# A convolution and SwiGLU kernel: a new order around the first pair of token blocks, and an earlier store in the last

## The chip, the cores and the metric

The kernel runs on one core of one Trainium2 chip. The metric is the device time of one execution, in microseconds (us). Times inside an execution are counted from the start of the profiled span.

## The reference

The input x has 8 sequences of 4096 tokens and 192 features. Eight heads of 24 features each have seven taps, a softmax over seven weights. The causal convolution feeds a SwiGLU feed-forward network without bias:

```python
w = softmax(weight)                                   # 8 heads x 7 taps
y[b, s, head] = sum(w[head, k] * x_pad[b, s + k, head] for k in range(7))
xn = y / sqrt(mean(y * y) + 1e-6) * rms_g             # per token, 192 features
g, val = xn @ w_gate, xn @ w_val                      # 192 -> 1536 each
out = (g / (1 + exp(-g)) * val) @ w_out               # 1536 -> 192
```

The network's weights arrive as 64-bit floats, so the kernel rebuilds 32-bit floats from pairs of words itself.

## The kernel before

**Pairs.** The 32768 tokens are worked through as 32 pairs, each of two blocks (g = 0, 1) of 512 tokens. The 1536 hidden features are 12 groups of 128, f, in four units of three. Pairs 1 to 31 use fewer, larger products: sums of weight tiles (`WSUM`, on GpSimd, written into `wf`) meet sums of inputs (`XSUM`, on VectorE, written into `xc`, L667), and the results are combined on ScalarE, VectorE and GpSimd. The same is done for the output product with sums of output weight tiles (`out_sums`, L811). Their instruction order is written out by hand in `ORDER`; a letter ahead of each name gives the engine.

**Pair 0** is computed plainly, because the sums are not there yet. `plain` makes 24 products (L981); for each of them ScalarE takes the silu of one half (L991, "silu step") and VectorE multiplies it with the other (L998, "value step"), which frees the two PSUM banks of the product. `outer` then multiplies with the output weights `wo_sb` (L1021): block 0 first takes f = 0 to 8 for four groups of 128 tokens, then f = 9 to 11, then block 1 takes all f. ScalarE and VectorE move the sums out (L1029, L1033).

**Conversion.** `convert` rebuilds weights in steps: three short operations on VectorE (L287, L291, L294), two or three on ScalarE (L298, L299, L302), one on VectorE (L304), and then, for the output weights, two on GpSimd (L310, L311), or, for the input weights, four more on VectorE up to L319. The output weights come in six parts of two f each; even parts share one scratch buffer, odd parts the other, so part i + 2 begins after part i has left GpSimd.

**The order around the first pair** is written in two tables. In `START` each letter takes one step: `p`, `s` and `v` a product, a silu and a value step of pair 0; `i` a step of an input weight unit; `o` and `O` a step of an even or odd output weight part; `c` a tap of pair 1's convolution; `n` a step of pair 1's normalisation (square on ScalarE, reduction on VectorE L470, factor on GpSimd L476 to L482, spread on VectorE L489, scaling on GpSimd L497); `w` a chunk of three or four weight sums (L345, L349). `LATER` places what is left between the instructions of `outer`, by a count in which one of its matmuls is 37.5; `t` stores pair 1's normalised input to DRAM from SyncE, and `fetch(1)` reads it back in the layout of the products. A place only fixes the order on each engine's queue; engines wait for each other by semaphores.

**Pair 2's** convolution in the version before is `conv(2)`: seven full-width taps on VectorE (L418, L420) into `y`. From pair 3 on `part_tap` is used: ScalarE puts the first tap of a third of the width into a free PSUM bank (L436), VectorE adds the others there (L444), the last one writing to `y`. After the last tap the buffer of x is free for the next `load`.

**The end of a pair.** Each half of a pair's output (rows of block 0, `st0`, and block 1, `st1`) is transposed on VectorE (`T11`, `T12`; `T21`, `T22`; L897) and stored with three transfers from SyncE (L947). In `ORDER`, `T21` and `st1` carry a "-": they run inside the following pair's list, and for the last pair behind `T11` and `st0`.

Of the kernel before, what the change touches and what calls it, by code (L numbers as in the profile page):

```python
# [19 lines left out]
def kernel(  # L20
# [10 lines left out]
    nc = tc.nc  # L31
# [391 lines left out]
        if k == K - 1:  # L423
            x_sb.pop(p)

    acc = {}

    def part_tap(p, k, j):

        cut = slice(j * T, (j + 1) * T)  # L430
        xf = x_sb[p][:].rearrange("p t a -> p (t a)")
        xk, w = xf[:, k * GS + j * T : k * GS + (j + 1) * T], tp[:, k : k + 1]
        if k == 0:
            h = SIDE[j]
            acc[p, j] = h, pick(h, False)
            nc.scalar.mul(bank(*acc[p, j])[:], xk, w)  # L436
            return
        at = bank(*acc[p, j])[:]
        dst = at
        if k == K - 1:  # L440
            if p not in ys:
                ys[p] = yp.tile([P, NJ, D], F32, name="y")
            dst = ys[p][:].rearrange("p j d -> p (j d)")[:, cut]
        nc.vector.scalar_tensor_tensor(  # L444
            out=dst, in0=xk, scalar=w, in1=at, op0=ALU.mult, op1=ALU.add
        )
        if k == K - 1:
            h, i = acc.pop((p, j))
            free[h].append(i)
            if not any(q == p for q, _ in acc):  # L450
                x_sb.pop(p)

    yn, st = {}, {}
# [237 lines left out]
    def put(at, do):  # L691
        heapq.heappush(line, (at, next(tick), do))
# [131 lines left out]
    class Pair:  # L824
        def __init__(self, p):
            self.p = p
            self.units = [Unit(u) for u in range(NU)]
            self.bk, self.tl, self.o_sb = {}, {}, {}
            self.line = self.products()

        def h(self, g, f):
# [80 lines left out]
        def do(self, eng, name):  # L912
            act, *at = name.split(".")
            p, n = self.p, NM * P
            if len(at) == 2:
                self.units[int(at[1])].do(eng, act, int(at[0]))
            elif at:
                self.sum(int(act[1]), int(at[0]), eng)
            elif act == "c1":
                self.open("Y", True)  # L920
                copy(eng, self.some("Y"), self.some("X"))
            elif act in ("s7", "c2"):
                t = self.tl[act] = tiles.pop(0)
                copy(eng, t[:, 0:n], self.some("Z" if act == "s7" else "X"))
            elif act in ("C22", "C21"):
                t = self.tl["s7" if act == "C22" else "c2"][:, 0:n]
                b = "X" if act == "C22" else "Z"
                nc.vector.tensor_tensor(out=t, in0=self.some(b), in1=t, op=ALU.add)
                if b == "Z":
                    self.close(b)  # L930
            elif act in ("T22", "T21"):
                t = self.tl.pop("s7" if act == "T22" else "c2")
                self.turn(t, 1, int(act[2]) - 1)
                tiles.append(t)
            elif act in ("T11", "T12"):
                b = "Y" if act == "T11" else "X"
                self.turn(self.bank(b), 0, int(act[2]) - 1)
                self.close(b)
            elif act in ("st0", "st1"):
                g = int(act[2])  # L940
                r = p * PT + g * T
                o = self.o_sb.pop(g)[:].rearrange("p a d -> p (a d)")
                o = o.rearrange("p (b d) -> p b d", d=HP)
                for c, rows, lo, hi in ((0, LOW, 0, 8), (1, UPP, 0, 8), (2, slice(0, P), 8, 12)):
                    n = T // (hi - lo)
                    to = out[r : r + T, c * HP : (c + 1) * HP].rearrange("(b p) d -> p b d", p=n)
                    nc.sync.dma_start(out=to, in_=o[rows, lo:hi, :])  # L947
            else:
                self.ahead(eng, act)

# [144 lines left out]
    def done(it):  # L1095
# [7 lines left out]


    START = (
        "XxxxxxXDdDdDTDdadTbTaTfbTakTakTakTkbkKkKkKkbkbfpoffpfsicpsvivOpsipiscvpisvpvwsicwpvs"
        "iwpvscwpsiwvpiscvipsvovpwispvswcipvwspsiwOvpsiwvipsvvpswopsvwcpsOnwonvpovnopOnOnopsOov"
    )
    LATER = (
        (-9, "t"), (54, "o"), (163, "s"),  # L1110
        (233, "s"), (294, "v"), (303, "s"), (463, "w"),
        (603, "v"), (679, "O"), (742, "w"), (802, "v"),
        (816, "O"), (1017, "O"), (1302, "w"), (1582, "w"), (1861, "w"), (2141, "w"),
        (2421, "w"),
    )
    conv_first(3, hot={4: 2, 5: 2, 6: 1})
    load(1)
# [29 lines left out]
    def later(it, *places):  # L1147
        for at in places:
            put(at, functools.partial(next, it, None))
# [10 lines left out]
        for at in places:  # L1160
            put(at, functools.partial(next, it, None))

    later(conv(2), *[c + 250 + 200 * i for i in range(K)], c + 1640)
    later(norm(2), c + 1650, c + 1850, c + 2050, c + 2420, c + 2440)
    later(place(2), c + 2450)
    xat = [c + i for i in (1660, 1730, 2060, 2130, 2200, 2270, 2340)]
    xat += [base + i for i in (2900, 2970, 3040, 3110, 3180)]
    for i, at in enumerate(xat[0 : len(XSUM)]):
        put(at, functools.partial(x_sum, i))
    later(out_sums(), *[base + 2600 + 60 * i for i in range(4 * NM)])  # L1170
    emit(float("inf"))
# [48 lines left out]
```

## Time and profile before

| | |
|---|---|
| three runs | 2630.27, 2627.51, 2630.32 us; median 2630.27 |
| profiled execution | 2624.07 us, of which the profiled span is 2622.2 |
| granted TensorE clock | 0.998 of full |
| PE, VectorE, ScalarE, GpSimd busy | 98%, 86%, 62%, 80% of the span |
| first plain product, first output product of pair 0, steady run of pair 1 begin | 38.9, 103.9, 145.45 us |
| last matmul ends | about 2614.7 us |

A line of a timeline gives start, duration, engine, source line, operation, output and inputs, count, and in brackets the idle time before it with what ended it. A line of the waits gives who waited for whom, the total, how often, and the longest. PE is TensorE, DVE VectorE, ACT ScalarE, POOL GpSimd, SPq the queue of SyncE. A matmul in 32-bit floats shows as two records.

### The profile page before, as it was taken

How to read it: one execution, taken by the hardware profiler on the slowest of the kernel's cores; microseconds unless marked ns; L12 is line 12 of the kernel's file. 1: busy time of each engine (PE TensorE's matmuls, PEld its weight loads, DVE VectorE, ACT ScalarE, POOL GpSimd, SP SyncE). 2: the span in 40 equal slices, each digit the busy share in tenths (PEclk: the TensorE clock that was granted, in tenths of full speed). 3: DMA queues.
4: the chain of work that ended last, by engine and by line, in shares of the span. 5: the costliest groups of instructions: out<-in, count | busy, mean ns of one | idle time of the engine just before them, and what ended most of it. 6: DMA issues, size and time to landing. Idle time of an engine off the chain costs nothing.

```text
span 2622.2 us, 71005 instructions
## 1 busy us (share of the span) xinstructions
PE 2579.8 (98%) x29002; PEld 1858.8 (71%) x29002; DVE 2268.0 (86%) x3606; ACT 1614.9 (62%) x2964; POOL 2091.7 (80%) x1693
## 2 busy tenths in 40 slices
PE   6899999999999999999999999999999999999998
PEld 4677777777777777777777777777757767777776
DVE  8988888888889888898888888888898888888875
ACT  5365556765557755567655567655577555676554
POOL 3988888777888777888788887778887778887776
PEclk9999999999999999999999999999999999999999
DMA  6313322323313233213233223233132332232210
GB/s 143 56 33 63 63 42 47 56 45 63 63 32 57 47 54 63 49 40 63 39 63 63 40 49 50 51 63 59 34 59 46 56 63 44 45 61 41 50 38 14
DMA packets 510659, 138.01 MB, mean 53 GB/s; under 512 B 482300, under 2 KB 484860, under 8 KB 510205
## 3 DMA queue, kind: packets, MB, share of 16 engines
q1 hardware_dynamic: 509772, 133.44, 27.1%
q8 instruction: 227, 3.72, 0.6%
q14 instruction: 100, 0.82, 0.1%
q10 hardware_dynamic: 560, 0.03, 0.0%
HBM read 83.87 MB, written 49.55 MB: 51 GB/s over the span
## 4 chain that ended last, share of the span: by engine, by line
PE 95%; POOL 1%; DMA 1%; DVE 1%; SPq 1%; issue 0%; ACT 0%; DVEq 0%; POOLq 0%
PE ps L753 62%; PE ps L882 33%; POOL wf L349 1%; PE ps L981 1%; DMA xh<-in_x_dram 0%; SPq L1119 0%; SPq L217 0%; DMA x<-in_x_dram 0%; POOL wo_sb L311 0%; DVE y L420 0%; DMA ht<-in_moe_w_val_dram 0%; DVE xc L667 0%; DVE ht L998 0%; DMA ht<-in_moe_w_gate_dram 0%; POOL xc L310 0%
## 5 line engine op out<-in xcount | busy, mean ns | idle before, releaser
L753 PE MATMUL ps<-xc,wf 64*128 64x512 f32 x4960 | 1253.8, 592 | 0.9 <-DVE xc L667 0.9
L753 PEld LDWEIGHTS ps<-xc,wf 64*128 64x128 f32 x4960 | 753.5, 186 | 315.5 <-issue 92.9
L753 PE MATMUL ps<-xb,wf 64*128 64x512 f32 x2480 | 711.2, 589 | 0.0
L705 ACT ACTIVATE tls<-ps 128x512 f32<-128x512 f32 (+1 forms) x636 | 365.7, 589 | 374.2 <-PE ps L882 203.1
L797 POOL TENSOR_TENSOR ht<-ht,tile 128x512 f32<-128x512 f32 x295 | 375.3, 1279 | 274.6 <-ACT tile L790 272.5
L705 ACT ACTIVATE tile<-ps 128x512 f32<-128x512 f32 x697 | 400.1, 594 | 269.3 <-PE ps L753 157.6
L753 PEld LDWEIGHTS ps<-xb,wf 64*128 64x128 f32 x2480 | 389.7, 187 | 146.5 <-issue 41.1
L705 ACT ACTIVATE ps<-ps 128x512 f32<-128x512 f32 (+1 forms) x651 | 366.9, 578 | 53.4 <-PE ps L882 38.8
L910 POOL TENSOR_TENSOR early<-ht 128x512 f32<-128x512 f32 x279 | 379.2, 1364 | 4.9
L797 POOL TENSOR_TENSOR ht<-ht,tls 128x512 f32<-128x512 f32 x201 | 255.2, 1277 | 72.5 <-ACT tls L790 70.6
L882 PE MATMUL ps<-ht,wo_sb 128*32 128x256 f32 (+1 forms) x6944 | 309.5, 326 | 0.0
L777 DVE TENSOR_TENSOR tile<-ps,tile 128x512 f32<-128x512 f32 x373 | 254.8, 686 | 56.3 <-PE ps L753 53.6
L444 DVE SCALAR_TENSOR_TENSOR ps<-xh,tp,ps 128x512 f32<-128x512 f32 x435 | 301.5, 744 | 1.0
L882 PEld LDWEIGHTS ps<-ht,wo_sb 128*32 128x32 f32 x6944 | 215.2, 110 | 93.2 <-POOL ht L797 22.7
L882 PE MATMUL ps<-ht,x 128*32 128x256 f32 (+1 forms) x5952 | 249.9, 326 | 0.6 <-issue 0.6
L910 POOL TENSOR_TENSOR ht<-ht 128x512 f32<-128x512 f32 x186 | 248.1, 1349 | 0.0
L790 ACT ACTIVATE tile<-tile 128x512 f32<-128x512 f32 x373 | 233.1, 629 | 12.5 <-DVE tile L777 12.5
L882 PEld LDWEIGHTS ps<-ht,x 128*32 128x32 f32 x5952 | 190.1, 110 | 54.7 <-issue 2.3
L777 DVE TENSOR_TENSOR ht<-ps,tls 128x512 f32<-128x512 f32 x311 | 211.5, 680 | 0.0
L777 DVE TENSOR_TENSOR ht<-ps,tile 128x512 f32<-128x512 f32 x309 | 210.1, 680 | 0.1
L777 DVE TENSOR_TENSOR tls<-ps,tls 128x512 f32<-128x512 f32 x247 | 169.2, 685 | 28.3 <-PE ps L753 26.1
L882 PE MATMUL ps<-early,x 128*32 128x256 f32 (+1 forms) x4464 | 193.1, 326 | 0.1
(129 smaller groups left out, 3164.6 us busy)
## 6 DMA issues: line engine op xcount, KB each, us to landing
xb<-xd SPq DMA_DIRECT2D x124, 384.0 KB
xd<-yn SPq DMA_DIRECT2D x248, 96.0 KB
out_dram<-o_sb SPq DMA_DIRECT2D x186, 128.0 KB
xh<-in_x_dram SPq DMA_DIRECT2D x192, 105.0 KB
xh<-in_x_dram SPq DMA_DIRECT2D x56, 98.4 KB
ht<-in_moe_w_gate_dram SPq DMA_DIRECT2D x12, 192.0 KB
ht<-in_moe_w_val_dram SPq DMA_DIRECT2D x12, 192.0 KB
tls<-in_moe_w_out_dram SPq DMA_DIRECT2D x8, 192.0 KB
```

The costliest lines, as they stand in the source:

```text
L349: nc.gpsimd.tensor_tensor(out=t[:, d, :], in0=t[:, a, :], in1=t[:, b, :], op=ALU.add if op == "add" else ALU.subtract,)
L444: nc.vector.scalar_tensor_tensor(out=dst, in0=xk, scalar=w, in1=at, op0=ALU.mult, op1=ALU.add)
L705: nc.scalar.activation(out=dst, in_=src, func=AF.Copy, scale=float(s))
L753: nc.tensor.matmul(out=self.new(v, h, True) if first else self.old(v, h), lhsT=wf[self.u][HALF[h], WAT[i], :], rhs=x_op(XOP[i])[HALF[h]], ...
L777: nc.vector.tensor_tensor(out=self.hv(v) if h else t[:], in0=self.old(v, h), in1=t[:], op=plus(s))
L790: nc.scalar.activation(out=t[:], in_=src[:], func=AF.Silu)
L797: engine[eng].tensor_tensor(out=self.hv(v), in0=src, in1=t[:], op=ALU.mult)
L882: nc.tensor.matmul(out=self.bank(b)[i * Q : (i + 1) * Q, at : at + n], lhsT=left, rhs=cols, start=fresh, stop=True, skip_group_check=True, ...
L910: engine[eng].tensor_tensor(out=dst, in0=a, in1=b, op=op)
L981: nc.tensor.matmul(out=bank(h, bks[h])[:], lhsT=wf[u][HALF[h], k * NF + f, :], rhs=xb[HALF[h], g, k, :], start=(k == 0), stop=(k == KP - 1 ...
```

## The change

Four things are changed. The order in `START` and `LATER`: one tap of pair 1 is moved behind the last conversion step of unit 1 and one behind that of unit 2; the value steps 18 to 23 come earlier among the conversions of the output weights; the weight sums from unit 2's second chunk on move behind all six parts of the output weights and then follow each other closely; the scaling of pair 1 moves behind output part 4. The convolution of pair 2 uses `part_tap`, with two thirds of the width first and the last third after them. The x sums of pair 1 are all placed ahead of the second evacuation group of `outer`, with pair 2's reduction and factor behind the seventh. For the last pair alone `T22`, `T21` and `st1` are done as soon as the second half's sum is there, and one transfer in three goes out from ScalarE.

The sets `ended` and `past` serve the bookkeeping while the instructions are emitted: x is released after the third part's last tap, and a name that was done early is skipped later.

```diff
@@ -423,7 +423,7 @@
         if k == K - 1:
             x_sb.pop(p)
 
-    acc = {}
+    acc, ended = {}, {}
 
     def part_tap(p, k, j):
 
@@ -447,7 +447,8 @@
         if k == K - 1:
             h, i = acc.pop((p, j))
             free[h].append(i)
-            if not any(q == p for q, _ in acc):
+            ended[p] = ended.get(p, 0) + 1
+            if ended[p] == len(SIDE):
                 x_sb.pop(p)
 
     yn, st = {}, {}
@@ -826,6 +827,7 @@
             self.p = p
             self.units = [Unit(u) for u in range(NU)]
             self.bk, self.tl, self.o_sb = {}, {}, {}
+            self.past = set()
             self.line = self.products()
 
         def h(self, g, f):
@@ -912,6 +914,9 @@
         def do(self, eng, name):
             act, *at = name.split(".")
             p, n = self.p, NM * P
+            if name in self.past:
+                return
+            self.past.add(name)
             if len(at) == 2:
                 self.units[int(at[1])].do(eng, act, int(at[0]))
             elif at:
@@ -928,6 +933,10 @@
                 nc.vector.tensor_tensor(out=t, in0=self.some(b), in1=t, op=ALU.add)
                 if b == "Z":
                     self.close(b)
+                    if p == PAIRS - 1:
+                        for name in ("T22", "T21", "st1"):
+                            if name not in self.past:
+                                self.do(eng, name)
             elif act in ("T22", "T21"):
                 t = self.tl.pop("s7" if act == "T22" else "c2")
                 self.turn(t, 1, int(act[2]) - 1)
@@ -944,7 +953,8 @@
                 for c, rows, lo, hi in ((0, LOW, 0, 8), (1, UPP, 0, 8), (2, slice(0, P), 8, 12)):
                     n = T // (hi - lo)
                     to = out[r : r + T, c * HP : (c + 1) * HP].rearrange("(b p) d -> p b d", p=n)
-                    nc.sync.dma_start(out=to, in_=o[rows, lo:hi, :])
+                    q = nc.scalar if c == 1 and p == PAIRS - 1 else nc.sync
+                    q.dma_start(out=to, in_=o[rows, lo:hi, :])
             else:
                 self.ahead(eng, act)
 
@@ -1103,15 +1113,13 @@
 
 
     START = (
-        "XxxxxxXDdDdDTDdadTbTaTfbTakTakTakTkbkKkKkKkbkbfpoffpfsicpsvivOpsipiscvpisvpvwsicwpvs"
-        "iwpvscwpsiwvpiscvipsvovpwispvswcipvwspsiwOvpsiwvipsvvpswopsvwcpsOnwonvpovnopOnOnopsOov"
+        "XxxxxxXDdDdDTDdadTbTaTfbTakTakTakTkbkKkKkKkbkbfpoffpfsicpsvivOpsipisvicpsvpvwsicwpvs"
+        "iwpvscwpsiwvpisvicpsvovpwispvswcipvwspsiwOvpsiwvipsvvpswopsvcpsvOnovnpsovnopsOvnOopsOoon"
     )
     LATER = (
-        (-9, "t"), (54, "o"), (163, "s"),
-        (233, "s"), (294, "v"), (303, "s"), (463, "w"),
-        (603, "v"), (679, "O"), (742, "w"), (802, "v"),
-        (816, "O"), (1017, "O"), (1302, "w"), (1582, "w"), (1861, "w"), (2141, "w"),
-        (2421, "w"),
+        (60, "t"), (163, "s"), (200, "v"), (250, "O"), (294, "v"), (330, "O"), (420, "O"),
+        (463, "w"), (564, "w"), (664, "w"), (764, "w"), (864, "w"), (964, "w"), (1064, "w"),
+        (1164, "w"), (1264, "w"),
     )
     conv_first(3, hot={4: 2, 5: 2, 6: 1})
     load(1)
@@ -1160,12 +1168,17 @@
         for at in places:
             put(at, functools.partial(next, it, None))
 
-    later(conv(2), *[c + 250 + 200 * i for i in range(K)], c + 1640)
-    later(norm(2), c + 1650, c + 1850, c + 2050, c + 2420, c + 2440)
+    for j in range(len(SIDE)):
+        put(c + 240 + 700 * (j // 2), functools.partial(part_tap, 2, 0, j))
+        for k in range(1, K):
+            at = c + 250 + 100 * k + 50 * j if j < 2 else c + 960 + 80 * k
+            put(at, functools.partial(part_tap, 2, k, j))
+    put(c + 1500, functools.partial(load, 3))
+    later(norm(2), c + 1510, c + 2300, c + 2310, c + 2420, c + 2440)
     later(place(2), c + 2450)
-    xat = [c + i for i in (1660, 1730, 2060, 2130, 2200, 2270, 2340)]
-    xat += [base + i for i in (2900, 2970, 3040, 3110, 3180)]
-    for i, at in enumerate(xat[0 : len(XSUM)]):
+    xat = [c + i for i in (1660, 1730, 2060, 2130, 2200, 2270, 2290)]
+    xat += [c + i for i in (2360, 2370, 2380, 2390)]
+    for i, at in enumerate(xat):
         put(at, functools.partial(x_sum, i))
     later(out_sums(), *[base + 2600 + 60 * i for i in range(4 * NM)])
     emit(float("inf"))
```

## The prediction

> **What bounds the kernel now.** I read the page's engine totals, then its chain of waits, then PE's waits over the whole run, then the timelines of the stretch in which those waits lie and of the last 20 us.
>
> ```profile
> PE 2579.8 (98%) x29002; PEld 1858.8 (71%) x29002; DVE 2268.0 (86%) x3606; ACT 1614.9 (62%) x2964; POOL 2091.7 (80%) x1693
> PE 95%; POOL 1%; DMA 1%; DVE 1%; SPq 1%; issue 0%; ACT 0%; DVEq 0%; POOLq 0%
> ```
>
> PE is the bound: the chain is PE from 145.45 us to 2614.7 us with no gap longer than 0.26 us. None of the edits removes a matmul, so time can only come from ahead of 145.45 us or from behind 2614.7 us. PE's waits say how much is there:
>
> ```profile
> PE ps L1021 <- POOL wo_sb L311: 3.3, 2, 1.7
> PE ps L1021 <- DVE ht L998: 3.0, 1, 3.0
> PE ps L981 <- DVE wf L319: 2.0, 2, 1.1
> PE ps L753 <- DVE xc L667: 0.9, 1, 0.9
> ```
>
> PE's own timeline places the L1021 and L753 waits between 105 and 146 us, where the first pair's output product runs:
>
> ```profile
> 103.92 1.46 PE L1021 MATMUL ps<-wo_sb,ht 64*128 64x192 f32 x8
> 108.34 1.89 PE L1021 MATMUL ps<-wo_sb,ht 64*128 64x192 f32 x18 [2.96 <-DVE ht L998]
> 111.90 9.70 PE L1021 MATMUL ps<-wo_sb,ht 64*128 64x192 f32 x116 [1.67 <-POOL wo_sb L311]
> 123.27 19.93 PE L1021 MATMUL ps<-wo_sb,ht 64*128 64x192 f32 x239 [1.68 <-POOL wo_sb L311]
> 145.45 1.13 PE L753 MATMUL ps<-xc,wf 64*128 64x512 f32 x4 [0.90 <-DVE xc L667]
> ```
>
> A record costs 83.5 ns here (9.70/116, 19.93/239). The first wait is for a PSUM bank: eight records go to the lower half, then the upper half needs the bank that value step 20 (L998) frees, and that step is late in VectorE's queue. The two others are for output weight parts 4 and 5 (f = 8 and f = 10). GpSimd's timeline shows what stands ahead of part 5:
>
> ```profile
> 110.23 1.62 POOL L311 TENSOR_TENSOR wo_sb<-xc 128x384 f32<-128x384 f32 x1
> 111.80 4.12 POOL L349 TENSOR_TENSOR wf<-wf 128x128 f32<-128x128 f32 x5
> 115.99 2.50 POOL L345 TENSOR_SCALAR wf<-wf 128x128 f32<-128x128 f32 x2
> 118.45 2.28 POOL L310 TENSOR_TENSOR xc<-xc,tls 128x384 f32<-128x384 f32 x1
> ```
>
> Seven weight sums, 6.3 us, run before it. On VectorE one short conversion runs beside GpSimd's scaling of pair 1 (L497, 102.83 to 105.67):
>
> ```profile
> 102.90 2.98 DVE L287 TENSOR_SCALAR xc<-tls 128x384 uint32<-128x384 uint32 x1 [1.83 <-POOL wo_sb L311]
> 106.88 0.35 DVE L294 TENSOR_SCALAR xc<-tls 128x384 uint32<-128x384 uint32 x1
> ```
>
> Alone such an operation takes 0.35 us. At the end, VectorE's and SyncE's timelines show the second half of the last pair's output waiting for the first:
>
> ```profile
> 2609.02 0.56 DVE L928 TENSOR_TENSOR tls<-ps,tls 128x384 f32<-128x384 f32 x1 [0.72 <-PE ps L882]
> 2614.80 0.65 DVE L897 STREAM_TRANSPOSE o_sb<-ps 128x256 f32<-128x256 f32 x2 [1.30 <-PE ps L882]
> 2615.37 0.59 DVE L897 STREAM_TRANSPOSE o_sb<-tls 128x256 f32<-128x256 f32 x2
> 2615.28 4.00 SPq L947 DMA_DIRECT2D out_dram<-o_sb  x6
> ```
>
> The data of that half are ready at 2609.6; its transpose runs at 2615.4 and its stores are the last three of six.
>
> **What the skill says.** The Trainium skill, "SBUF — State Buffer", section "SBUF: two separate sides": VectorE and GpSimd share a port pair as an exclusive lock held for a whole instruction, which an operation in a two-port mode or with two SBUF inputs needs. The trace agrees: 2.98 us instead of 0.35 while the 2.84 us scaling ran. So an operation moved on GpSimd also moves a block on VectorE. The Trainium skill, "DMA: Bandwidth & Descriptors", section "Issuing engines are not separate DMA queues": issuing from a second engine saves only issue time. The trace of before has all six stores on one queue, so nothing in it tests this.
>
> **The change part by part.** Durations are of the profiled execution: span 2622.2, own time 2624.07 us. The median of the runs is 2630.27, so 6.2 us is added at the end for whatever differs between the two.
>
> *One tap of pair 1 put behind the unit's last conversion, for units 1 and 2.* These remove the two L319 waits (0.86 and 1.15 us). VectorE is full there (20.0 of 20 us between 60 and 80), so the tap of 2.0 us only lands on the next value steps, and PE needs their banks: value step 3 ends at 58.1 instead of 58.0, and value steps 9 and 10 end about 0.9 us later. After unit 3's conversion both orders have done the same work. I take 0.4 us of the 2.0; bounds 0 and 1.3. The output product starts at 103.5 instead of 103.9.
>
> *Value steps 18 to 21 ahead of the conversions.* Step 20 now stands ahead of part 3's conversion, and its silu ahead of part 2's on ScalarE; it ends near 98.5. The 2.96 us wait goes. Late next is part 4: PE reaches f = 8 after 26 records, 2.2 us, at 105.7.
>
> *Weight sums and scaling behind parts 2 to 4.* Part 2 ends as before (102.9): it hangs on the factor step (L476 to L482, 2.5 us), still ahead of it. From there: GpSimd's first half of part 3, 1.0, blocks VectorE; three conversions of part 4, 1.05; L304, 0.55; then GpSimd's L311 of part 3, L310 and L311 of part 4, 1.0 each: 108.5. PE waits 2.8 us and resumes at 108.6 instead of 111.90: 3.3 us. Part 5 now has one operation, the scaling, ahead: 2.8 plus 2 x 1.0, done near 114, against PE's need at 118.4. The 1.68 us wait goes. PE would end the product at 108.6 + 358 x 0.0835 = 138.5.
>
> *What the later scaling holds up.* It runs from 108.9 to 111.8, not 102.8 to 105.7: 6.1 us later. SyncE's eight stores of pair 1 (5.2 us) and its four fetches wait for it in turn. The last fetch lands at about 121.9 before (DMA is busy until there), so at 128.0 now. VectorE's x sums cannot start earlier. Before, they start at 127.16, behind the taps, so here a hidden transfer comes into view.
>
> *Taps of pair 2 through PSUM.* Before: 1.17 + 1.97 + 1.95 + 8.75 = 13.8 us of VectorE. Now 18 at 0.743 (L444) = 13.4, and three first taps on ScalarE at 0.68 (L436), idle there. They start at 110 to 113 and end at 123 to 127, before the fetch lands, so they cost nothing; with the fetch on time they would be the limit. SyncE's load of pair 3 waits for them, behind the fetch in its queue; nobody needs it before 195.
>
> *x sums.* Eleven, 0.67 to 0.94 each, say 0.8: 8.8; one output addition 0.54; the reduction of pair 2, now in their midst, 1.75 + 0.24 + 0.22: 11.5 in all, so 139.5 (138.5 to 140.6). Then VectorE's spread (0.24) and one addition (0.53), which frees the upper bank that pair 1's second product takes: 140.35 instead of 145.45. **Front: 5.1 us**, bounds 3 and 7.
>
> *The 34 weight sums behind part 5.* At 0.47 alone and with 0.05 between, 17.7 us: 114 to 132, and 2 more beside the x sums. The factor step, 2.5 us, follows the reduction, which ends near 136.3, and the spread needs it at 139.5: no room to spare. Twelve output sums and the second scaling then end near 149.5; pair 1's first GpSimd product came 10.9 us after that pair's start, so about 151. Hidden.
>
> *Last pair.* Both transposes and the store move to 2609.6, where VectorE idles until 2612.8. After 2615.28 three stores are left instead of six: two on SyncE at 0.6 to 0.65, one on ScalarE, whose issues at the start took 0.39 to 0.72. Last issue ends near 2616.6 instead of 2619.28. **Tail: 2.6 us**, bounds 2.0 and 2.8. ScalarE has nothing behind it.
>
> Steady pairs keep their order, banks and durations: nothing. Sum: 7.7 us; profiled execution 2616.4, median 2630.27 - 7.7 = **2622.6**.
>
> **Rivals.** *PE stays the limit.* If the scaling is not blocked and the fetch lands at 126, pair 1 starts when the product ends, 138: front 7.4, in all 10.0, 2620.3. For it: before, the scaling took 2.84 us, unblocked, and 2 us gained on this chain suffice. Against: every step from 102 to 112 alternates on the shared lock. 15%.
>
> *The fetch becomes the bound.* Scaling or fetch come 3 us later still, because VectorE takes the lock between GpSimd's operations or load 3 shares the DMA engines (they are 0.7 to 0.9 busy with it in the trace): front 2.1, in all 4.7, 2625.6. 17%.
>
> *Slower: the weight sums hold VectorE.* They now stand ahead of pair 2's factor step, and VectorE's spread waits for that with the bank-freeing additions of pair 1 behind it. They took 0.84 each between 123.2 and 136.7, beside two-input taps, and up to 1.13. At 1.1 they end at 151.4; with 2.3 for the factor and 0.9 behind, pair 1 starts at 154.6, 9.1 late: 6.5 slower, 2636.8. It decides from 0.91 us each. Against it: the new taps read one input from PSUM, and the steady pairs' GpSimd sums beside them took 1.36 for 1.28. 8%.
>
> **Numbers.** The main case has 60%. A difference within 0.2%, 5.3 us, is about what a measurement of this kernel can tell from no change. Main and PE cases are faster by more (75%, and 2% of the fetch case), the rest of the fetch case lies within, the last is slower. The range goes from the PE case, less 2 for the scatter of a median, to the fetch case, plus 2: 2618 to 2627.5.
>
> **What would show it.** PE's timeline after: no wait for ht at L1021, one for part 4 of 2 to 3.5 us ending near 108.6, none for part 5; the scaling near 109; x sums idle until 128 for DMA; pair 1's second product near 140.4; six stores split three and three, the span ending 2.6 us behind what the front gives. Wrong would be: x sums starting by 125, a spread waiting on GpSimd beyond 141, or a wait in a steady pair.

## The result, and the profile after

| | before | after |
|---|---|---|
| median of 13 runs each (range), us | 2625.54 (2623.11 to 2630.32) | 2621.67 (2617.74 to 2623.89) |
| ratio of times, 95% interval | | 0.9981 [0.9973, 0.9989] |
| profiled execution; span, us | 2624.07; 2622.2 | 2620.28; 2618.4 |

The change makes the kernel faster by 1.1 to 2.7 thousandths, 2.9 to 7.1 us of 2625.5; the bound of 0.2% from the prediction lies inside this interval, so whether the gain exceeds it, as the prediction had it, stays open. The two medians lie 3.9 us apart, the two profiled executions 3.8. The predicted time was 2622.6. That it lies only 0.9 us from the measured median is luck, because two errors cancel: the median of 2630.27 that it started from came out at 2625.54 over more runs, and the gain of 7.7 us came out at 3.9 (5.0 by the ratio). From 2625.54 the same gain would have given 2617.8, just below the stated range.

In the kernel after, the lines of the file have moved: the products are L754 (L753 before), the output product of the pairs is L884 (L882), the plain product L991 (L981), `outer` L1031 (L1021), the x sums are L668 (L667), the value step L1008 (L998), spread, factor and scaling L490, L483 and L498, `outer`'s additions L1043, the last transposes L899 (L897), the stores L957 (L947).

Engine totals and shares of the chain, from the page of the kernel after:

```profile
PE 2580.3 (99%) x29002; PEld 1866.1 (71%) x29002; DVE 2265.0 (87%) x3617; ACT 1617.3 (62%) x2967; POOL 2079.0 (79%) x1693
PE 96%; DVE 2%; DMA 1%; issue 0%; POOL 0%; ACT 0%; SPq 0%; DVEq 0%; POOLq 0%; ACTq 0%
```

PE does the same 29002 records in 0.5 us more. GpSimd has fallen out of the chain (1% before). PE's waits over the whole run:

```profile
PE ps L884 <- issue: 3.3, 5, 1.4
PE ps L1031 <- POOL wo_sb L311: 2.5, 2, 1.4
PE ps L754 <- DVE xc L668: 1.1, 1, 1.1
PE ps L754 <- ACT tile L706: 0.3, 1, 0.3
```

The 3.0 us for `ht` and the 2.0 for `wf` are gone, and the waits for output parts fell from 3.3 to 2.5. But the steady pairs' output product (L884) now waits 3.3 us for nothing that the profile shows ("issue"), and there is a new wait of 0.3 us for ScalarE, in pair 3. Before, the only wait in the steady pairs was this one:

```profile
PE ps L882 <- issue: 1.9, 5, 0.8
```

PE's timeline between 102 and 142 us, after:

```profile
102.67 1.62 PE L1031 MATMUL ps<-wo_sb,ht 64*128 64x192 f32 x15
105.67 0.92 PE L1031 MATMUL ps<-wo_sb,ht 64*128 64x192 f32 x8 [1.38 <-POOL wo_sb L311]
107.72 29.36 PE L1031 MATMUL ps<-wo_sb,ht 64*128 64x192 f32 x355 [1.12 <-POOL wo_sb L311]
139.49 1.09 PE L754 MATMUL ps<-xc,wf 64*128 64x512 f32 x2 [1.07 <-DVE xc L668]
140.87 0.69 PE L754 MATMUL ps<-xc,wf 64*128 64x512 f32 x1 [0.28 <-DVE o_sb L1043]
```

PE stops for part 3 (1.38) and part 4 (1.12), not for part 5: 355 records run through in one piece, 82.7 ns each, from 107.72, where before they resumed at 111.90 and stopped again at 121.6. The second product of pair 1 reaches its upper half at 140.87 instead of 145.45. The other engines in the same stretch:

```profile
107.62 3.00 POOL L498 TENSOR_TENSOR yn<-y,s 128x1536 f32<-128x1536 f32 x1
107.80 3.03 DVE L294 TENSOR_SCALAR xc<-tls 128x384 uint32<-128x384 uint32 x1
110.64 6.36 SPq L633 DMA_DIRECT2D xd<-yn  x8
118.98 2.60 SPq L646 DMA_DIRECT2D xb<-xd  x4
129.61 0.93 DVE L668 TENSOR_TENSOR xc<-xb 128x512 f32<-128x512 f32 x1 [4.09 <-DMA xb<-xd]
138.67 0.68 DVE L668 TENSOR_TENSOR xc<-xc 128x512 f32<-128x512 f32 x1
140.13 0.25 DVE L490 STREAM_TRANSPOSE s<-s 128x64 f32<-128x64 f32 x1 [0.78 <-POOL s L483]
140.29 0.98 DVE L1043 TENSOR_TENSOR o_sb<-ps,o_sb 128x384 f32<-128x384 f32 x2
```

This is the chain that now sets pair 1's start: scaling, eight stores, four fetches, the first x sum after 4.09 us in which VectorE has nothing to do, the last x sum ending at 139.35, the spread after 0.78 us for the factor, and the addition that frees the bank. How much of the gain is still there one stage later is read from the chain of waits, at the step where pair 1's output product begins; first before, then after:

```profile
196.57 27.44 PE ps L882 x672
```

```profile
191.96 27.44 PE ps L884 x672
```

At this point after is 4.6 us ahead. VectorE's and the issuing queues' timelines at the end:

```profile
2607.68 0.64 DVE L899 STREAM_TRANSPOSE o_sb<-tls 128x256 f32<-128x256 f32 x2
2608.16 6.46 SPq L957 DMA_DIRECT2D out_dram<-o_sb  x4
2608.16 5.83 ACTq L957 DMA_DIRECT2D out_dram<-o_sb  x2
2612.87 0.65 DVE L899 STREAM_TRANSPOSE o_sb<-ps 128x256 f32<-128x256 f32 x2 [1.30 <-PE ps L884]
```

The second half's transpose runs 5.2 us ahead of the first half's instead of behind it, and four stores are on SyncE, two on ScalarE. The last matmul starts 5.88 us ahead of the span's end, before 7.74: 1.9 us. Front and tail make 6.5 us; the spans differ by 3.8. So 2.7 us were given back between 192 and 2612 us, in pairs whose work the change doesn't touch.

### The profile page after: what moved, and what is told of

It is laid out like the page before. It is cut to its first block, busy times and chain, and to the rows that moved or that the text cites. A ratio compares the mean times of both kernels' runs of the same rounds, so it can differ in the third digit from the quotient of the medians.

```text
span 2618.4 us, 71028 instructions
## 1 busy us (share of the span) xinstructions
PE 2580.3 (99%) x29002; PEld 1866.1 (71%) x29002; DVE 2265.0 (87%) x3617; ACT 1617.3 (62%) x2967; POOL 2079.0 (79%) x1693
## 4 chain that ended last, share of the span: by engine, by line
PE 96%; DVE 2%; DMA 1%; issue 0%; POOL 0%; ACT 0%; SPq 0%; DVEq 0%; POOLq 0%; ACTq 0%
PE ps L754 62%; PE ps L884 33%; PE ps L991 1%; PE ps L1031 1%; DMA x<-in_x_dram 0%; DMA xb<-xd 0%; DVE y L405 0%; DVE ht L1008 0%; DVE y L420 0%; DVE y L393 0%; DVE xc L304 0%; PE ps L594 0%; DVE wf L319 0%; ACT xb L614 0%; DVE xc L668 0%
## 5 line engine op out<-in xcount | busy, mean ns | idle before, releaser
L754 PE MATMUL ps<-xc,wf 64*128 64x512 f32 x4960 | 1252.8, 592 | 1.6 <-DVE xc L668 1.1
L754 PEld LDWEIGHTS ps<-xc,wf 64*128 64x128 f32 x4960 | 760.9, 186 | 308.1 <-issue 88.8
L754 PE MATMUL ps<-xb,wf 64*128 64x512 f32 x2480 | 709.1, 589 | 0.0
L754 PEld LDWEIGHTS ps<-xb,wf 64*128 64x128 f32 x2480 | 392.9, 187 | 141.2 <-issue 38.7
L444 DVE SCALAR_TENSOR_TENSOR ps<-xh,tp,ps 128x512 f32<-128x512 f32 x450 | 312.1, 745 | 1.7 <-ACT ps L436 0.6
L884 PE MATMUL ps<-ht,wo_sb 128*32 128x256 f32 (+1 forms) x6944 | 310.5, 326 | 0.0
L884 PEld LDWEIGHTS ps<-ht,wo_sb 128*32 128x32 f32 x6944 | 216.3, 110 | 92.8 <-POOL ht L798 23.5
L884 PE MATMUL ps<-ht,x 128*32 128x256 f32 (+1 forms) x5952 | 250.1, 326 | 0.4 <-issue 0.4
L884 PEld LDWEIGHTS ps<-ht,x 128*32 128x32 f32 x5952 | 190.5, 110 | 54.2 <-issue 1.6
L884 PE MATMUL ps<-early,x 128*32 128x256 f32 (+1 forms) x4464 | 193.5, 326 | 0.0
## 6 DMA issues: line engine op xcount, KB each, us to landing
out_dram<-o_sb SPq DMA_DIRECT2D x184, 128.0 KB
```

Of the source, the lines that this page charges most:

```text
L444: nc.vector.scalar_tensor_tensor(out=dst, in0=xk, scalar=w, in1=at, op0=ALU.mult, op1=ALU.add)
L754: nc.tensor.matmul(out=self.new(v, h, True) if first else self.old(v, h), lhsT=wf[self.u][HALF[h], WAT[i], :], rhs=x_op(XOP[i])[HALF[h]], ...
L884: nc.tensor.matmul(out=self.bank(b)[i * Q : (i + 1) * Q, at : at + n], lhsT=left, rhs=cols, start=fresh, stop=True, skip_group_check=True, ...
```

## The experiments

For every run I take four numbers from PE's records. *Front* is the time from the first plain product (38 to 39.5 us in all) to pair 1's first output product. *Start* is the time from the first plain product to the upper half of pair 1's second product, the point that the prediction put at 140.35. *Stops* is what lies between PE's records over their usual spacing, whatever its cause, from pair 1's first output product to the last matmul. *Tail* is the time from the last matmul's start to the end of the span. Where the start is left out, the product runs on without a gap at that point.

| run | own time, us | front | start | stops | tail |
|---|---|---|---|---|---|
| before | 2624.07 | 157.6 | 106.5 | 5.9 | 7.74 |
| after | 2620.28 | 153.1 | 102.0 | 8.5 | 5.88 |
| e1 tail only | 2622.68 | 157.4 | 106.3 | 7.3 | 5.88 |
| e2 front only | 2625.17 | 154.6 | 101.9 | 10.3 | 7.77 |
| e3 reduction early | 2617.41 | 150.5 | | 8.7 | 5.89 |
| e4 and load 3 later | 2620.32 | 150.5 | | 11.0 | 5.90 |
| e5 one queue | 2621.24 | 152.4 | 101.3 | 9.7 | 5.70 |
| e6 full taps | 2629.72 | 161.0 | 108.5 | 10.1 | 5.91 |
| e7 weight sums early | 2620.84 | 152.5 | 101.4 | 10.0 | 5.90 |
| e8 scaling early | 2624.62 | 155.7 | | 10.4 | 5.90 |
| e9 taps only | 2624.83 | 156.1 | | 7.9 | 7.65 |
| e10 swap undone | 2623.43 | 153.4 | 102.4 | 10.9 | 5.90 |
| e11 value steps undone | 2622.69 | 152.4 | 101.4 | 11.8 | 5.90 |
| e12 best | 2617.27 | 148.5 | | 9.7 | 5.91 |

After, e2 and e5 have the same front, instruction for instruction: it takes 152.4 to 154.6, and the start lies at 101.3 to 102.0. Part of e2's 154.6 is the clock, which was granted at 0.70 and 0.63 from 140 to 145 us where after had 1.00. So a difference of 0.7 us in the start, or of some 2 in the front, tells nothing unless a wait explains it.

**e1, the tail alone.** Before, with the hunks `past`, the early `T22`, `T21`, `st1`, and the second queue:

```diff
+                    if p == PAIRS - 1:
+                        for name in ("T22", "T21", "st1"):
...
-                    nc.sync.dma_start(out=to, in_=o[rows, lo:hi, :])
+                    q = nc.scalar if c == 1 and p == PAIRS - 1 else nc.sync
+                    q.dma_start(out=to, in_=o[rows, lo:hi, :])
```

> The order of before at the front, with only the last pair's early transposes, early store and the transfer from ScalarE. Theory (the gain is a sum of a front of 4.6 us and a tail of 1.9 us, less small stops of PE in the steady pairs that belong to the execution and not to the change): pair 1's first output product starts at 196.6 as before; from the start of the last transposes of block 0 to the end of the span 5.5 us instead of 7.4; time 1.9 us less, ratio 0.9993; the stops in pairs 2 to 31 add up to anything between 5 and 9 us. Rival (the change itself makes the steady pairs 2.6 us longer, through the banks that pair 2's taps leave behind): the stops are 5.8 us as before, since the banks are those of before.

Measured: median of 13 runs 2623.50 against 2626.0, ratio 0.9990 [0.9982, 0.9999]; tail 5.88 against 7.74.

**e2, the front alone**, is the kernel after with these hunks taken out:

> The new order and the taps in PSUM, with the last pair as before. Theory: pair 1's first output product at 192.0, the last transposes to the end of the span 7.4 us, time 4.6 us less than before give or take 2 (ratio 0.9975 to 0.999), stops in pairs 2 to 31 anything between 5 and 9 us. Rival (the front makes the steady pairs longer): stops 8.3 us again, and only 2 us left of the gain.

Measured: 2623.27 in the median of 13, ratio 0.9990 [0.9982, 0.9998]; the start 4.6 us earlier than before, the stops 10.3. The stops lie above the 5 to 9 of the theory, on the rival's side. Each part alone is worth about 1.0 thousandth, and the two together 1.9, as if they added. The times say no more than that: e1 gains 0.3 to 4.7 us by its interval, where the tail gives 1.9, and e2 0.5 to 4.7, where the start gives 4.6.

**e3, the reduction moved into VectorE's idle stretch.** If the fetch is what VectorE waits for, the reduction of pair 2 (1.75 us and two short ones) costs nothing in the 4.1 us ahead of the x sums and 2.2 us in their midst.

```diff
-    later(norm(2), c + 1510, c + 2300, c + 2310, c + 2420, c + 2440)
+    later(norm(2), c + 1510, c + 1655, c + 2310, c + 2420, c + 2440)
```

> After, with pair 2's reduction (L471 to L473, 2.2 us of VectorE) ahead of the first x sum, into the 4.1 us in which VectorE waits for the fetch. Theory (the chain scaling, stores, fetch, x sums, spread sets the start of pair 1): the last x sum ends at 137.6 instead of 139.35, the spread no longer waits for the factor, the second product's upper half starts near 138.6 instead of 140.87, pair 1's first output product at 189.7 instead of 191.96, 2.3 us less than after. Rival (PE or GpSimd set the start of pair 1 and the x sums only seem to): the output product stays within 0.5 us of 191.96.

VectorE's timeline of e3, then PE's:

```profile
126.29 1.75 DVE L471 TENSOR_REDUCE s<-yn 128x64 f32<-128x1536 f32 x1 [1.13 <-ACT yn L460]
128.57 0.69 DVE L668 TENSOR_TENSOR xc<-xb 128x512 f32<-128x512 f32 x1
```

```profile
136.91 1.56 PE L754 MATMUL ps<-xc,wf 64*128 64x512 f32 x6
```

The reduction lies where VectorE idled, the x sums start at 128.57 without a wait, and pair 1's first six records stand in one group from 136.91, where after they are torn apart until 140.87. The front is 2.5 us shorter; 2617.19 in the median of six runs, ratio to before 0.9968 [0.9957, 0.9980]. **e4** adds to it that the load of pair 3 leaves SyncE only behind the first place stores of pair 2, since in the profile after its packets run beside the last of the fetch:

```diff
-    put(c + 1500, functools.partial(load, 3))
+    put(base + 2000, functools.partial(load, 3))
```

> As the one with the early reduction, and pair 3's load behind the first store of pair 0 in SyncE's queue, so that it does not share the DMA engines with pair 1's fetch. Theory (the load's packets, which come between the fetch's from 127 us on, delay its landing by 1.5 us): the first x sum starts near 128.0 instead of 129.6, the last ends near 136.0, and PE itself is the limit: pair 1 starts as soon as the output product of pair 0 ends, 137.4, and the output product of pair 1 starts at 188.7, 3.2 us less than after. Rival (the fetch's own issue and transfer set its landing): the first x sum stays at 129.6 and the output product at 189.7 as with the early reduction alone.

Measured: the same front, 150.5, and ratio 0.9969 [0.9956, 0.9981]. The x sums start right behind the reduction in both (e4: at 129.37), so their start can't say whether the load slows the fetch. The packets can: the fetch has 768 of 2 KB, and from its first issue to the end of its last packet it takes 9.50 us in e4, where the load's packets come only afterwards, and 9.35 in after, where they begin 1.0 us before the fetch is through. Over all profiles it is 8.9 to 9.5 without the load beside it and 9.0 to 9.4 with it. The load does not slow the fetch.

**e5, all six stores on SyncE's queue** (`q = nc.sync`):

> After, with all of the last pair's stores on SyncE. Theory (behind the last matmul the end is set by the transfer of three stores that arrive together, not by their issue): from the last matmul's start to the end of the span 5.9 us as after, within 0.2. Rival (the issue is what counts, as the prediction reckoned): 6.5 us, one issue of 0.65 more.

Measured: tail 5.70 against 5.88. ScalarE's queue earns nothing. It does save issue time: the last issue ends 2.08 us behind the start of the last matmul in after, and 2.78 in e5. But the last packet ends 2.57 us behind the last issue in after, and 1.67 in e5, so the transfer takes back the 0.70 us. This agrees with what the prediction cited of the skill, that a second engine saves issue time only.

**e6, pair 2's taps at full width as before**, all else as after. This tests the slower rival, which needed weight sums of 0.91 us each.

```diff
-    for j in range(len(SIDE)):
-        put(c + 240 + 700 * (j // 2), functools.partial(part_tap, 2, 0, j))
...
-    put(c + 1500, functools.partial(load, 3))
+    later(conv(2), *[c + 250 + 200 * i for i in range(K)])
```

> After, with pair 2's convolution as seven full-width taps on VectorE. Theory (the taps themselves lie beside the fetch, but with two SBUF inputs they contend with GpSimd's 34 weight sums, and those now stand ahead of the factor step for which VectorE's spread waits): the weight sums take 0.8 each and end near 140 instead of 131.7, the spread ends near 143, the second product's upper half starts 2 to 5 us later than 140.87. Rival (where the taps accumulate costs nothing, since VectorE waits for the fetch anyway): 140.87 within 0.5.

GpSimd's, VectorE's and PE's timelines of e6:

```profile
116.12 14.04 POOL L349 TENSOR_TENSOR wf<-wf 128x128 f32<-128x128 f32 x13
131.57 11.56 POOL L349 TENSOR_TENSOR wf<-wf 128x128 f32<-128x128 f32 x17
146.61 0.24 DVE L490 STREAM_TRANSPOSE s<-s 128x64 f32<-128x64 f32 x1 [5.79 <-POOL s L483]
147.35 1.22 PE L754 MATMUL ps<-xc,wf 64*128 64x512 f32 x1 [4.34 <-DVE o_sb L1043]
```

Thirteen weight sums take 14.0 us where the same thirteen after take 6.5. These are means over different neighbours. For the weight sums that run beside taps alone, the view of line 349 gives count, then shortest, median and longest in ns; first e6, then after:

```profile
L349 POOL TENSOR_TENSOR wf<-wf x5: 1847/1852/1971, 116.1 to 124.0; 128x128 f32<-128x128 f32 x5
```

```profile
L349 POOL TENSOR_TENSOR wf<-wf x21: 450/457/462, 114.0 to 125.0; 128x128 f32<-128x128 f32 x21
```

Beside full-width taps of 1.9 us, GpSimd gets one weight sum done per tap, and the sum takes as long as the tap. Beside taps that read PSUM it takes 0.46 us, as it does in e6 once the taps are over. Beside e6's x sums, which again read two inputs from SBUF, it takes 0.8 to 0.9. The factor is late, the spread waits 5.8 us for it, and PE 4.34 for the addition behind the spread. All 34 lie between 116.1 and 144.1, 0.82 each in the mean. The start is 6.5 us later than after and 2.0 later than before, the front 8.0 and 3.4, the rest of it at a lower clock behind the long wait. That is more than the 1.8 of the tail: with two-input taps the slower rival's mechanism eats the whole gain. The span, 2627.9, is 5.7 us over that of before, but 4.2 of this are stops, so the one run doesn't say how much slower this kernel is in the mean.

**e7, the weight sums back ahead of part 5**, two chunks in `LATER` and two in `START`:

```diff
-vpswopsvcpsvOnovnpsovnopsOvnOopsOoon
+vpswopsvwcpsvOnwovnpsovnopsOvnOopsOoon
...
-(330, "O"), (420, "O"), (463, "w"), (564, "w"),
+(330, "O"), (340, "w"), (350, "w"), (420, "O"),
```

> After, with four chunks of unit 2's weight sums put back ahead of output weight parts 1, 2 (its factor step) and 5. Theory (the gain of the front comes from the value steps ahead of the conversions and from the scaling behind part 4; GpSimd sat idle 3.4 us before the factor step, and part 5 has 4 us to spare): PE resumes for part 4 within 0.5 us of after (68.9 us behind the first plain product), no wait for part 5 or one below 0.5, and pair 1's first output product stays within 0.7 us of after (153.1 us behind the first plain product). Rival (the weight sums ahead of the parts are what PE waited for): part 4 comes 2 us later or more, and the wait of 1.7 us for part 5 is back.

Measured: no wait for part 5; 1.90 for part 3 and 1.14 for part 4, 3.0 against 2.5 after; the start at 101.4, within the scatter of the same front. Moving the weight sums earned nothing that this run can show, and part 5 is in time without it.

**e8, the scaling back where the factor ends**, ahead of parts 3 and 4:

```diff
-OvnOopsOoon
+OvnnOopsOoo
```

> After, with the scaling of pair 1 on GpSimd ahead of output weight part 3, as before. Theory (the scaling's place trades the weight parts against the fetch): PE's waits for parts 3 and 4 grow by 2.8 us, the first x sum comes at 125.5 to 126 instead of 129.6 right behind the taps, the wait for x sums goes, and pair 1's first output product moves by less than 1 us. Rival (the fetch is no limit, the weight parts alone are): the output product comes 2.8 us later.

PE's timeline, then PE's clock in two stretches (start:end, length, busy and records of PE, granted clock, share of the DMA engines, GB/s; the view's columns of the other engines lie between), then VectorE's timeline:

```profile
107.94 0.92 PE L1031 MATMUL ps<-wo_sb,ht 64*128 64x192 f32 x8 [3.92 <-POOL wo_sb L311]
109.98 32.23 PE L1031 MATMUL ps<-wo_sb,ht 64*128 64x192 f32 x355 [1.12 <-POOL wo_sb L311]
```

```profile
110.00:115.50 5.50, 5.50 (x34) 5.50 (x36) 4.81 (x10) 3.18 (x6) 3.63 (x6) 0.50 0.52 125
115.50:120.00 4.50, 4.50 (x56) 4.50 (x56) 4.50 (x8) 0.00 (x0) 3.95 (x10) 0.96 1.05 222
```

```profile
125.74 0.98 DVE L668 TENSOR_TENSOR xc<-xb 128x512 f32<-128x512 f32 x1
```

The trade is as the theory has it: the x sums start at 125.74 right behind the taps, with no wait for DMA, and PE's wait for part 3 grows by 2.5 us. That would be even. But the wait of 3.92 us is followed by half clock from 110.0 to 115.5, and the 355 records take 32.23 us instead of 29.36: 2.87 us, about the 2.7 by which the front is longer. So the front moves by the rival's number, 2.8, but for another reason; without the slower clock it would be 152.9 by these figures, an estimate, against 153.1 after.

**e9, the taps in PSUM alone**, put into the kernel before:

```diff
-    later(conv(2), *[c + 250 + 200 * i for i in range(K)], c + 1640)
+    for j in range(len(SIDE)):
+        put(c + 240 + 700 * (j // 2), functools.partial(part_tap, 2, 0, j))
...
+    put(c + 1640, functools.partial(load, 3))
```

> Before, with pair 2's taps in PSUM and nothing else. Theory (the taps' place matters through GpSimd: with one input from PSUM they leave the shared port to it): output weight part 5 takes 1.0 and 1.0 on GpSimd instead of 2.3 and 2.4, the weight sums 0.5 each instead of 0.84, PE's wait of 1.7 for part 5 goes, VectorE's spread no longer waits 3.3 for the factor, and pair 1's first output product comes 2 to 3.5 us earlier (154 to 155.5 us behind the first plain product instead of 157.6). Rival (as the prediction reckoned, the taps cost and gain nothing): 157.6 within 0.3.

GpSimd's and PE's timelines, and PE's clock:

```profile
121.20 8.64 POOL L349 TENSOR_TENSOR wf<-wf 128x128 f32<-128x128 f32 x16
111.45 31.79 PE L1022 MATMUL ps<-wo_sb,ht 64*128 64x192 f32 x355 [0.43 <-POOL wo_sb L311]
```

```profile
108.00:115.00 7.00, 6.07 (x40) 5.57 (x42) 6.41 (x12) 4.08 (x10) 6.62 (x10) 0.61 0.46 101
115.00:120.00 5.00, 5.00 (x56) 5.00 (x54) 5.00 (x9) 1.04 (x3) 1.05 (x2) 0.86 1.00 230
```

The sixteen weight sums take 8.6 us where before they took 13.5. The wait for part 5 is gone, the spread waits 0.25, and the front is 1.5 us shorter, less than the 2 to 3.5 expected. After a wait of 2.95 us for `ht` the granted clock falls to 0.61, and the 355 records take 2.43 us longer than after. Without that the front could be up to 3.9 us shorter, an estimate: the last x sum ends at 142.69, just ahead of pair 1's first products, and might have been waited for. Time: 2624.91 in the median of 12, ratio 0.9993 [0.9985, 1.0002], not told apart from no change.

**e10, the tap order undone** in both places of `START`, and **e11, the value steps undone**:

```diff
-vivOpsipisvicpsvpvwsicwpvs
+vivOpsipiscvpisvpvwsicwpvs
...
-iwpvscwpsiwvpisvicpsvovpwisp
+iwpvscwpsiwvpiscvipsvovpwisp
```

> After, with the two taps of pair 1 back ahead of the last conversions of units 1 and 2. Theory (the earlier products only lengthen PE's wait for the output weight parts): the output product of pair 0 starts 65.0 us behind the first plain product instead of 63.3, PE's waits for the parts shrink by as much, and pair 1's first output product stays at 153.05 within 0.5. Rival (the 1.7 us reach the end): 154.7.

```diff
-vcpsvOnovnpsovnopsOvnOopsOoon
+vcpsOnonvvpsonopsOnOopsOvoon
...
+(190, "v"),
```

> After, with the value steps 18 to 21 behind the conversions, about where they were before. Theory (the wait for the bank would end before that for part 4 does, so that the parts hide it): PE waits for a value step (L1008) until about 105, then for part 4 until about 108.2, and pair 1's first output product comes 0.3 to 1 us later than 153.05 behind the first plain product. Rival (the 2.96 us wait was worth its whole length, as the prediction reckoned): 2.5 us later or more.

PE's timelines of e10 and of e11:

```profile
106.67 0.92 PE L1031 MATMUL ps<-wo_sb,ht 64*128 64x192 f32 x8 [0.40 <-POOL wo_sb L311]
108.71 29.36 PE L1031 MATMUL ps<-wo_sb,ht 64*128 64x192 f32 x355 [1.12 <-POOL wo_sb L311]
```

```profile
104.33 1.89 PE L1031 MATMUL ps<-wo_sb,ht 64*128 64x192 f32 x18 [0.87 <-DVE ht L1008]
107.26 29.36 PE L1031 MATMUL ps<-wo_sb,ht 64*128 64x192 f32 x355 [1.04 <-POOL wo_sb L311]
```

In e10 the output product starts 1.6 us later against the first plain product, but the wait for part 3 shrinks from 1.38 to 0.40, and the start comes 0.3 us later than after. In e11 PE waits 0.87 for the value step, then 1.04 for part 4, and resumes at 107.26, no later than after. This is not the wait of before: the step ends 3.8 us earlier against the first plain product than it did there, since the conversion ahead of it (L287) takes 1.16 us, and before took 2.98 beside the scaling, which now comes later. Both starts lie within or near the scatter of the same front: each of these two parts, undone alone, is worth less than a run of this kind can show. What one gives, the wait for the next part takes.

**e12, the version that follows from this.** e3, and in `START` the last two steps of part 2 ahead of pair 1's reduction and factor, with the spread behind the first step of part 4: if parts 2 to 4 are what PE waits for, they should pass GpSimd earlier.

```diff
-vcpsvOnovnpsovnopsOvnOopsOoon
+vcpsvOnovoonpsvnpsOvOonpsOoon
...
-    later(norm(2), c + 1510, c + 2300, c + 2310, c + 2420, c + 2440)
+    later(norm(2), c + 1510, c + 1655, c + 2310, c + 2420, c + 2440)
```

> After with the early reduction of pair 2, and with output weight part 2 converted ahead of pair 1's reduction and factor, its spread behind part 4's first step. Theory (part 2 waits on GpSimd for a factor step it does not need, and parts 3, 4, the scaling and the fetch hang on it): PE's waits for parts 3 and 4 shrink from 2.5 to below 0.5 us, the scaling starts near 105.5 instead of 107.3, pair 1's first output product comes 1.5 to 2.4 us earlier than with the early reduction alone (148.1 to 149 us behind the first plain product instead of 150.5). Rival (the fetch and the x sums stay the limit): 150.5 within 0.5.

GpSimd's and PE's timelines of e12:

```profile
106.07 2.99 POOL L498 TENSOR_TENSOR yn<-y,s 128x1536 f32<-128x1536 f32 x1
106.17 29.36 PE L1031 MATMUL ps<-wo_sb,ht 64*128 64x192 f32 x355 [0.74 <-POOL wo_sb L311]
135.74 1.56 PE L754 MATMUL ps<-xc,wf 64*128 64x512 f32 x6
```

PE waits only 0.74 us for the parts (below 0.5 was expected), the scaling starts at 106.07 instead of 107.62, and the front is 148.5: 2.1 less than e3 and 4.6 less than after. Median of five runs 2617.08, ratio to before 0.9962 [0.9948, 0.9975]. After had 0.9981 [0.9973, 0.9989]: the two intervals barely touch. So this version is faster than before, and with the shorter front very probably faster than after, against which it was not timed directly. From e3 (0.9968) it is not told apart by time.

**Where the 2.7 us go.** In the profile after, PE's timeline around one of the stops, and the DMA queues in the 2.9 us before it (packets, MB, share):

```profile
2197.81 1.26 PE L884 MATMUL ps<-nt,x 128*32 128x256 f32 x27
2200.43 0.95 PE L884 MATMUL ps<-nt,x 128*32 128x128 f32 x17 [1.36 <-issue]
```

```profile
q8 instruction: 1, 0.02, 2.6%
```

PE stands still for 1.36 us with no engine to wait for; shortly before, one packet of 16 KB of the instruction queue has ended. In the fourteen profiles, all 83 stops of over 0.4 us in an output product end 1.2 to 1.6 us after such a packet has ended. The queue has 227 packets in the whole run, about one for every 256 of PE's 58004 records of matmuls and weight loads, so it looks like PE's own. Most packets bring no stop. All 83 that do came when the DMA engines had been at least half busy for 3 us, which holds for only a third of all packets. The stops all lie in pairs 3 to 5, 11 to 13, 18, 19, 25 and 26, four to nine in a profile, and their lengths differ from run to run. So PE seems to wait for its instructions there when other transfers hold them up; that is a reading of the packets, and no run tested it. The sum of the stops is 5.9, 7.3 and 7.9 us in the three profiles with the old `START`, and 8.5 to 11.8 in the eleven with a new one, 10.1 in the mean: some 3 us more. About 0.7 us of that is no such stop: it recurs in pairs 3, 8, 30 and 31 with the same lengths in the nine profiles that have the new `START`, the late scaling and the taps in PSUM, and is missing in before and e1. Its largest piece, 0.28, goes with the wait of 0.25 us for ScalarE in pair 3. Why the new order has more of both stays open.

## Why the prediction was right or wrong

**The bound and the places of the gain: right.** PE stays the bound, the waits for `ht`, for `wf` and for part 5 are gone, and the gain lies ahead of pair 1 and behind the last matmul, as the sum put it. Predicted and seen: PE resumes at 108.6 (107.72), the scaling starts at 108.9 (107.6), the fetch lands at 128.0 (the first x sum starts at 129.61), the x sums idle for it (4.09 us), pair 1's second product takes its upper half at 140.35 (140.87). The front of 5.1 came out at 4.6. Part of this closeness is luck. The fetch's last packet ends at 128.32, near the predicted 128.0, because the scaling came 1.3 us earlier and the eight stores took 6.36 us instead of 5.2. The x sums then start 1.6 us late, but with the reduction and the addition among them they take 9.7 us instead of 11.5. One reading of the lines is a little off, and nothing rests on it: the seven weight sums ahead of part 5 take 6.6 us, not 6.3.

**"Steady pairs keep their order, banks and durations: nothing": the step that failed.** The order written for these pairs is the same, and still PE loses 2.7 us more in them in the profiled executions, some 3 in the mean of the profiles. It is the largest single error of the sum, and with 4.6 and 1.9 it accounts for the 3.8 between the spans. The prediction listed "a wait in a steady pair" as what would make it wrong, and this came: 0.25 us of it wait for ScalarE, and most of the rest has no engine behind it. The sign was in the profile before: the prediction reads its chain as having no gap longer than 0.26 us, but the row shown above has a stop of 0.8.

**"Tail: 2.6 us": mis-sized, 1.9.** I put the gain at the last issue, and that moved as foreseen: it ends 2.1 us behind the start of the last matmul, before 4.8. But the end is set by a transfer: the last issue ends at 2614.62, the last packet at 2617.19, 2.57 us behind it, and the span at 2618.4. Before, the last packet ended 1.68 us behind the last issue. With two queues it is 2.57 or 2.58 in all profiles, with one 1.59 to 1.70, so the closer the issues, the longer the transfer behind the last of them, and 0.9 us of the saving are lost.

**"Swap of taps: 0.4 us": mis-sized at its place, and worth little at the end.** The output product came 1.7 us earlier against the first plain product, not 0.4. But e10 shows that what it gains is waited for again at part 3, a wait that the prediction did not see: it took PE to run 26 records on to part 4, and PE stopped after 18. The two waits, 1.38 and 1.12, come to 2.5 together, near the 2.8 that I had put at part 4.

**"Value steps earlier: the 2.96 us wait goes": right in the trace, wrong as a gain.** e11 puts that wait back, at 0.87 us, and PE still resumes no later: parts 3 and 4 arrive when they arrive. So once the scaling is out of the way, the path at this place is the parts' way through GpSimd and not the value steps'; e12, which shortens that way and carries e3's reduction, resumes at 106.17. With the scaling early, as in e8, PE waits for part 3 until 69.4 us behind the first plain product, and before it waited for the value step until the same 69.4: there too the parts were as late.

**"Taps cost nothing": wrong by what they do to others.** The taps' own time was indeed hidden. But e6 and e9 show that their place decides how long GpSimd's work beside them takes: 0.46 us for a weight sum instead of 1.85 to 1.97, 1.0 for a step of part 5 instead of up to 2.4. Left at full width, they eat what this change gains; alone, they take part 5's wait away. The mean of 0.84 from which the prediction reckoned mixed sums beside taps, beside x sums and alone. I had this in the slower rival, as a reason against it, and should have had it in the sum: the taps are the part of the change without which the later weight sums don't pay.

**The rivals.** "PE stays the limit" was wrong: e3 gains 2.5 us by moving VectorE's work out of the x sums, so fetch and x sums set the start. "The fetch becomes the bound" is what happens in kind (4.09 us of waiting), at 1.6 us beyond the main case's landing instead of 3. The slower rival did not happen; e6 shows its cause at work once the taps are at full width, at 0.82 us per sum, under the 0.91 from which it was to decide, but the sums start at 116.1 and not at 114, and from there the same reckoning decides at 0.85. With the measured tail that is about even; the lower clock then makes it slower.

## What to carry to other kernels

When several waits stand in one stretch of the bounding engine, removing one moves the time to the next; the sum is to be made from the last producer (here the weight parts through GpSimd, and the fetch through SyncE), and single undos that cost nothing show which edits are not on it in the new order. An operation that costs nothing by its own time may still set the speed of another engine that shares its access to memory, so ask what runs beside it. For a transfer at the very end, count to its landing and not to its issue, and keep in the range that work which nobody touched can lose a few microseconds to a new alignment.

## What the runs showed of the hardware

**A wait of PE can be paid twice.** After 3.92 us (e8) the granted clock was 0.50 for 5.5 us, at a cost of 2.87 us; in e6, after 4.34 us, it was 0.67 from 147 to 152 us. The Trainium skill, "TensorE: Matmul & The Clock Gate", section "Part 1: The HAM clock gate (the "warmup" mystery)", gives an idle window of about 3.4 us for this, and these two agree. But the clock also fell after 2.95 us in e9, while before, after 2.96 us at the same place, it stayed at 1.00; and in e2 it fell to 0.63 after waits of only 0.75 and 0.28 us. So the length of the last wait alone does not say whether the clock will fall.

**Weight sums beside taps.** GpSimd's addition of 128 x 128 took 0.45 to 0.46 us beside VectorE's taps that read one input from PSUM (after, e9), and 1.85 to 1.97 beside taps of 1.9 us with both inputs in SBUF (before, e6): one addition per tap. This is the lock that the prediction cited, instruction by instruction. It shows again in after: a conversion that takes 0.35 us alone took 3.03 beside the 3.00 us of scaling.
